# MLP weight gradients into free K/V slots, the last group finished earlier, and the MLP ahead of head 2, in an attention-plus-MLP backward kernel

## The chip, the cores and the metric

The kernel runs on one core of one Trainium2 chip. The metric is device time in microseconds (us), the median over several executions. "Span" is the length of the one profiled execution as the trace shows it; it is about 2 us shorter than the device time of the same execution.

## The reference

One decode step (one token) of attention over a cached K and V, with an MLP (SwiGLU) beside it, and then the gradients with respect to all inputs. Cut to what matters:

```python
# x, grad_out: 1x1x640; k_cache, v_cache: 1x32x8192x128; wq: 640x4096; wo: 4096x640
# w1, w3: 640x1728; w2: 1728x640; all bfloat16
xn  = layernorm(x)
q   = xn @ wq                                  # 32 heads of 128
p   = softmax(q k^T * 128**-0.5);  o = p v
h   = silu(xn @ w1) * (xn @ w3)
out = x + o @ wo + h @ w2
outputs = (out, *vjp(grad_out))   # dx, dk_cache, dv_cache, dwq, dwo, dw1, dw3, dw2
```

With one token, every large gradient is an outer product of two vectors: dK and dV are 2 MB for each of 32 heads; dw1, dw3 and dw2 are 2.2 MB each. Nearly all the time goes into moving K and V in and dK and dV out: of 304 MB moved, the four make up 268.

## The kernel before

Per head h, `phase_a` makes the scores (transposes of K on TensorE) and the softmax, `phase_t` makes the products of V with dO on VectorE, and `phase_b` overwrites the K and V tiles with dK and dV and writes them out. Loads are issued by SyncE, writes of gradients by GpSimd. There are nine 2 MB slots; a load can be issued only when its slot is free, that is, when the dK or dV that filled it has been written out. At the start the MLP's weights hold four of the nine.

```python
    kvpool = ctx.enter_context(tc.tile_pool(name="kv", bufs=9))
    tpool = ctx.enter_context(tc.tile_pool(name="tp", bufs=3))
    # ... cut ...
    load_group(0)
    load_kv(4)                      # K0 V0 K1 V1
    mD = kv_tile("mD")              # w2
    mC = kv_tile("mC")              # remainders of w1, w3, w2
    mA = kv_tile("mA")              # w1
    mB = kv_tile("mB")              # w3
    # ... loads of w2, w1, w3 cut ...
    load_kv(1)                      # K2
    # ... cut ...
    def phase_b(h):
        # ... cut ...
        for lo in range(0, J, J // 2):
            outer(Vt, doh, P2, lo, lo + J // 2)       # VectorE, line L329
        nc.gpsimd.dma_start(dvc[h], Vt[:])            # L345
        for lo in range(0, J, J // 2):
            outer(Kt, qh, U2, lo, lo + J // 2)
        nc.gpsimd.dma_start(dkc[h], Kt[:])            # L348

    def finish_group(g):            # after every fourth head: dwo, dwq and parts of out and dx
        G_ = grp.pop(g)
        # ... cut: matmuls, products on VectorE ...
        nc.gpsimd.dma_start(dwo_v[:, g * GH:(g + 1) * GH, :], wo_g[:])
        # ... cut ...
        nc.gpsimd.dma_start(dwq_v[:, :, g * GW:(g + 1) * GW], wq_g[:])

    def mlp_grads():
        oA = kv_tile("oA")
        oB = kv_tile("oB")
        oC = kv_tile("oC")
        oD = kv_tile("oD")
        d1a, d3a, d1b, d3b, d2a, d2b = split_views(oA, oB, oC, oD)
        for wi in range(2):
            bc = make_bc(wi)        # broadcast of dgate / dup: VectorE, PE, ScalarE, four steps
            da, db, dv = ((d1a, d1b, dw1_v), (d3a, d3b, dw3_v))[wi]
            for ci in range(NA):
                nc.vector.tensor_scalar(da[:, ci, :], bc[:, 0:F], xn_col[:, ci:ci + 1], None, ALU.mult)
            nc.gpsimd.dma_start(dv[:, 0:NA, :], da)
            nc.vector.tensor_scalar(db, bc[:, 0:F], xn_col[:, NA:NC], None, ALU.mult)
            nc.gpsimd.dma_start(dv[:, NA, :], db)
        for b in range(NBA):        # 12 products of dw2
            nc.vector.tensor_scalar(d2a[:, b, :], g_bc[:], hcol[:, b:b + 1], None, ALU.mult)
        # ... cut: dw2's writes, and its two last products ...

    prep_group(0)
    for h in range(2):
        phase_a(h)
        phase_t(h)
        phase_b(h)
        load_kv(2)
        if h == 0:
            load_group(1)
    phase_a(2)
    mlp()
    load_kv(4)
    phase_t(2)
    for h in range(2, H):
        # ... cut: load and prepare the next group ...
        if h + 1 < H:
            phase_a(h + 1)
            phase_t(h + 1)
        phase_b(h)
        load_kv(2)
        if hh == GH - 1:
            finish_group(g)
    # ... cut: out and dx ...
    mlp_grads()
```

## Time and profile before

| | before |
|---|---|
| device time | 766.58 us, median of 3 (765.08 to 769.03) |
| span of the profiled run | 764.5 us |
| bytes moved, mean rate | 304.35 MB, 398 GB/s |
| busy: TensorE, VectorE, ScalarE | 79%, 72%, 42% |

Below, and in all listings: PE is TensorE, PEld its weight loads, DVE VectorE, ACT ScalarE, POOL GpSimd, SP SyncE; SPq is SyncE's DMA queue. A program line is written L329.

First, the page of the kernel before: the span in 40 equal slices (19.1 us each). A digit is the mean busy share of the 16 DMA engines in tenths; below it is the rate.

```profile
DMA  8999988999999999999999999999999999999668
GB/s 344 389 428 426 415 366 328 357 424 421 411 404 401 417 425 424 430 425 420 426 430 425 416 417 424 429 424 373 412 426 426 417 359 385 401 420 389 289 270 307
```

The middle is DMA-bound. Slices 6 to 8 (95 to 153 us) and the last three are weak. The windows view of the same kernel says it in one line each. Its columns are the window and its length, then busy time and number of instructions on five engines, the granted TensorE clock, the DMA share, and GB/s.

```profile
105.00:147.00 42.00, 34.00 (x682) 29.83 (x680) 34.65 (x51) 17.56 (x26) 2.90 (x5) 0.86 0.84 321
200.00:600.00 400.00, 330.85 (x5980) 282.46 (x5981) 300.29 (x409) 185.27 (x254) 28.81 (x48) 0.79 1.01 419
```

Cut finer, the front stretch shows an empty DMA at 112.5 us:

```profile
112.50:115.00 2.50, 2.50 (x74) 2.37 (x72) 2.13 (x2) 0.16 (x1) 0.35 (x1) 1.00 0.10 39
...
122.50:125.00 2.50, 2.50 (x76) 2.49 (x73) 2.14 (x6) 2.21 (x3) 0.00 (x0) 0.98 0.92 269
125.00:127.50 2.50, 2.50 (x33) 2.16 (x32) 2.50 (x3) 2.11 (x3) 0.00 (x0) 0.50 0.96 315
```

Two timelines of the kernel before tell why. Columns: start, duration, engine, line, operation. SyncE's queue issues the loads of K5 (92.02), V5 (99.62) and K6 (100.05), and then nothing until V6 at 121.46, which waits for the write of head 2's dV; GpSimd issues that write only at 114.64, because VectorE reaches head 2's products only when the MLP is done, at 99.8 us.

```profile
92.02 0.33 SPq L123 DMA_DIRECT2D Kt<-in_A_k_cache_dram  x1
...
100.05 0.82 SPq L123 DMA_DIRECT2D Kt<-in_A_k_cache_dram  x1
121.46 0.33 SPq L123 DMA_DIRECT2D Vt<-in_A_v_cache_dram  x1
```

```profile
114.64 0.53 POOL L345 DMA_DIRECT2D out_dram<-Vt  x1 [53.75 <-DVE Vt L329]
```

The tail has two holes. Between 705 and 712.5 us everything loaded has landed and head 30's dV is not made yet; at 737.5 to 743 us the MLP gradients start from nothing. From the windows view of the kernel before:

```profile
705.00:707.50 2.50, 2.50 (x15) 1.87 (x13) 1.11 (x3) 0.10 (x2) 0.00 (x0) 0.50 0.34 144
707.50:710.00 2.50, 1.94 (x20) 1.36 (x19) 2.50 (x4) 0.00 (x0) 0.00 (x0) 0.79 0.06 26
710.00:712.50 2.50, 1.57 (x63) 1.48 (x59) 2.50 (x5) 0.00 (x0) 0.00 (x0) 0.90 0.10 33
...
737.50:740.00 2.50, 1.43 (x3) 0.20 (x2) 1.34 (x4) 1.18 (x3) 0.00 (x0) 0.50 0.10 35
740.00:742.50 2.50, 0.16 (x1) 0.00 (x0) 2.50 (x6) 0.59 (x1) 0.38 (x1) 0.50 0.00 0
```

And GpSimd's timeline there: head 30's dV and the first write of dw3 (oB):

```profile
712.56 0.53 POOL L345 DMA_DIRECT2D out_dram<-Vt  x1 [13.58 <-DVE junk L313]
...
748.41 0.88 POOL L494 DMA_DIRECT2D out_dram<-oB  x1 [4.95 <-DVE oB L493]
```

### The profile page before, as it was taken

The numbers are of one execution on the slowest core, as the hardware profiler recorded it, in microseconds if no ns is written. First come the engines' busy times: TensorE is split into PE (matmuls) and PEld (weight loads), VectorE is DVE, ScalarE is ACT, GpSimd is POOL, SyncE is SP. The second block draws the span as 40 slices with busy tenths as digits, with TensorE's granted clock in tenths as the row PEclk, the third lists the DMA queues.
The fourth block names the chain that finished last, engine by engine and source line by source line (L and its number), as shares of the span: only waits on it lengthen the run. The fifth ranks groups of instructions, "written<-read, shape, count | busy, mean of one in ns | idle before, by whom it ended". The sixth has DMA issues, their size and how long they took to land. (4 is left out here: it accounts for less than half of the span.)

```text
span 764.5 us, 23388 instructions
## 1 busy us (share of the span) xinstructions
PE 601.9 (79%) x10637; PEld 504.7 (66%) x10637; DVE 550.9 (72%) x810; ACT 323.0 (42%) x452; POOL 54.0 (7%) x95
## 2 busy tenths in 40 slices
PE   5977899599569996969768897769969798699340
PEld 3845588588458885858658676658758676687220
DVE  1792697786488888856689567866788567987963
ACT  3704246275146652725518233544418235264030
POOL 0000000100001000100001000100001000100011
PEclk9965699696587998867868678776778868697555
DMA  8999988999999999999999999999999999999668
GB/s 344 389 428 426 415 366 328 357 424 421 411 404 401 417 425 424 430 425 420 426 430 425 416 417 424 429 424 373 412 426 426 417 359 385 401 420 389 289 270 307
DMA packets 35051, 304.35 MB, mean 398 GB/s; under 512 B 2840, under 2 KB 13912, under 8 KB 18568
## 3 DMA queue, kind: packets, MB, share of 16 engines
q1 hardware_dynamic: 21828, 151.35, 48.7%
q0 software_dynamic: 12960, 151.34, 47.5%
q8 instruction: 83, 1.36, 0.7%
q10 hardware_dynamic: 164, 0.17, 0.1%
q14 instruction: 16, 0.13, 0.0%
HBM read 151.51 MB, written 151.34 MB: 396 GB/s over the span
## 5 line engine op out<-in xcount | busy, mean ns | idle before, releaser
L261 ACT COPY KT<-pT 128x1024 bf16<-128x1024 bf16 x256 | 243.1, 1036 | 53.5 <-PE pT L259 51.3
L304 PE MATMUL dp<-T,ident_bf 128*128 128x256 bf16 x1024 | 190.5, 324 | 15.1 <-DVE T L302 15.0
L302 DVE TENSOR_TENSOR T<-Vt,do_g 128x2048 bf16<-128x2048 bf16 x128 | 154.3, 1216 | 42.0 <-DMA Vt<-in_A_v_cache_dram 28.3
L259 PE MATMUL pT<-ident_bf,Kt 128*128 128x128 bf16 x2048 | 168.9, 229 | 15.2 <-DMA Kt<-in_A_k_cache_dram 15.2
L259 PEld LDWEIGHTS <-Kt 128*128 128x128 bf16 x2048 | 130.9, 103 | 20.6 <-DMA Kt<-in_A_k_cache_dram 18.0
L304 PEld LDWEIGHTS <-ident_bf 128*128 128x128 bf16 x1024 | 107.5, 115 | 41.5 <-issue 16.7
L264 PEld LDWEIGHTS <-KT 128*128 128x128 bf16 x2048 | 79.1, 98 | 36.8 <-ACT KT L261 24.0
L264 PE MATMUL sA<-qc_g,KT 128*128 128x1 bf16 x2048 | 89.2, 165 | 13.5 <-ACT KT L261 4.9
L324 ACT COPY od_g<-sA 128x2 f32<-128x2 f32 x32 | 5.1, 161 | 189.6 <-PE sA L322 166.8
L322 PEld LDWEIGHTS <-Kt 128*128 128x128 bf16 x2048 | 59.6, 101 | 31.8 <-issue 30.2
L286 PEld LDWEIGHTS <-Vt 128*128 128x128 bf16 x2048 | 57.3, 98 | 19.3 <-issue 17.3
L345 POOL DMA_DIRECT2D out_dram<-Vt x32 | 17.6, 549 | 482.9 <-DVE junk L313 190.5
L235 ACT COPY KT<-pT 128x1024 bf16<-128x1024 bf16 (+1 forms) x24 | 19.8, 874 | 40.9 <-PE pT L233 40.9
L277 ACT ACTIVATE E<-sA,negM 128x64 f32<-128x64 f32 x32 | 10.3, 321 | 63.2 <-DVE negM L274 63.0
L307 DVE TENSOR_REDUCE DP<-dp 128x64 f32<-128x256 f32 x32 | 13.3, 416 | 23.1 <-PE dp L304 23.1
L348 POOL DMA_DIRECT2D out_dram<-Kt x32 | 17.3, 542 | 147.1 <-DVE negM L274 36.0
L317 DVE COPY negD<-sA 128x1 f32<-128x1 f32 x32 | 5.0, 155 | 30.3 <-PE sA L314 30.3
L233 PE MATMUL pT<-ident_bf,wo_g 128*128 128x128 bf16 x160 | 17.0, 279 | 7.4 <-DMA wo_g<-in_A_wo_dram 7.4
L378 ACT COPY KT<-pT 128x1024 bf16<-128x1024 bf16 (+1 forms) x24 | 19.3, 877 | 2.3 <-PE pT L376 2.2
L274 DVE COPY negM<-sA 128x1 f32<-128x1 f32 x32 | 4.9, 152 | 21.1 <-PE sA L271 21.0
L233 PEld LDWEIGHTS <-wo_g 128*128 128x128 bf16 x160 | 14.5, 129 | 8.3 <-DMA wo_g<-in_A_wo_dram 7.9
L314 PE MATMUL sA<-rdot,negones_f 128*128 128x1 f32 x64 | 13.6, 282 | 7.8 <-DVE junk L313 7.8
(392 smaller groups left out, 844.6 us busy)
## 6 DMA issues: line engine op xcount, KB each, us to landing
Kt<-in_A_k_cache_dram SPq DMA_DIRECT2D x32, 2048.0 KB, 21.2
Vt<-in_A_v_cache_dram SPq DMA_DIRECT2D x32, 2048.0 KB, 23.4
out_dram<-Vt POOLq DMA_DIRECT2D x32, 2048.0 KB, 15.1
out_dram<-Kt POOLq DMA_DIRECT2D x32, 2048.0 KB, 19.9
wq_g<-in_A_wq_dram SPq DMA_DIRECT2D x8, 640.0 KB, 27.3
wo_g<-in_A_wo_dram SPq DMA_DIRECT2D x8, 640.0 KB, 24.6
out_dram<-wo_g POOLq DMA_DIRECT2D x8, 640.0 KB, 20.3
out_dram<-wq_g POOLq DMA_DIRECT2D x8, 640.0 KB, 25.3
```

The source lines that it names most:

```text
L233: nc.tensor.transpose(pT[:, k, :], wo_g[:, hh, ci * P:(ci + 1) * P], ident_bf[:])
L235: nc.scalar.copy(wT[:, 0:len(bl), :], pT[:, 0:len(bl), :])
L259: nc.tensor.transpose(pT[:, k, :], K3[:, 8 * c + k, :], ident_bf[:])
L261: nc.scalar.copy(KT[:], pT[:])
L264: nc.tensor.matmul(sA[:, j:j + 1], lhsT=KT[:, k, :], rhs=qcol, start=(j == 0), stop=True, skip_group_check=True)
L286: nc.tensor.matmul(sA[:, OC:OC + 1], lhsT=V3[:, j, :], rhs=P2[:, j, 0:1], start=False, stop=(j == J - 1), skip_group_check=True)
L302: nc.vector.tensor_tensor(T3, V3[:, :, ds_], do_h[:, ds_].unsqueeze(1).to_broadcast([P, J, QD]), ALU.mult)
L304: nc.tensor.matmul(dp[:], lhsT=ident_bf[:], rhs=T3[:, :, R * i:R * (i + 1)], start=(q == 0 and i == 0), stop=(q == DH // QD - 1 and i == Q ...
L322: nc.tensor.matmul(sA[:, OC + 1:OC + 2], lhsT=K3[:, j, :], rhs=U2[:, j, 0:1], start=False, stop=(j == J - 1), skip_group_check=True)
L345: nc.gpsimd.dma_start(dvc[h], Vt[:])
L348: nc.gpsimd.dma_start(dkc[h], Kt[:])
L378: nc.scalar.copy(wT[:, 0:len(bl), :], pT[:, 0:len(bl), :])
```

## The change

Three parts, no operation added or removed. (1) The MLP goes ahead of head 2's `phase_a`, so that its four slots come free, and VectorE gets to head 2, earlier. (2) The MLP weight gradients use slots that no further load needs: dw1 after head 29, dw3 and dw2 after head 30. (3) The last `finish_group` goes ahead of the last head's outer products, so that the last thing written is head 31's dK. The diff, cut to its core:

```diff
-        G_ = grp.pop(g)
+        G_ = grp[g]
@@ the gradients, cut
-    def mlp_grads():
+    gt = {}
+    def grads_w(wi):
+        t = kv_tile("oW")
+        v = t[:, 0:NA * F].rearrange("p (c f) -> p c f", f=F)
+        bc = make_bc(wi)
+        if wi == 0:
+            gt["C"] = kv_tile("oC")
+        tb = gt["C"][:, wi * F:(wi + 1) * F]
+        dv = (dw1_v, dw3_v)[wi]
+        for ci in range(NA):
+            nc.vector.tensor_scalar(v[:, ci, :], bc[:, 0:F], xn_col[:, ci:ci + 1], None, ALU.mult)
+        nc.gpsimd.dma_start(dv[:, 0:NA, :], v)
+        nc.vector.tensor_scalar(tb, bc[:, 0:F], xn_col[:, NA:NC], None, ALU.mult)
+        nc.gpsimd.dma_start(dv[:, NA, :], tb)
+    def grads_w2():      # cut: as before, but the two last products and their writes come first
@@ the main loop
-    phase_a(2)
     mlp()
     load_kv(4)
+    phase_a(2)
     phase_t(2)
@@
+        if h == H - 1:
+            finish_group(g)
         phase_b(h)
         load_kv(2)
-        if hh == GH - 1:
+        if h == H - 3:
+            grads_w(0)
+        elif h == H - 2:
+            grads_w(1)
+            grads_w2()
+        if hh == GH - 1 and h < H - 1:
             finish_group(g)
@@
-    mlp_grads()
```

More of the change, by code (lines that the diff above doesn't have):

```diff
@@ L481, in mlp @@
                                      start=False, stop=True, skip_group_check=True)
-    def mlp_grads():
-        oA = kv_tile("oA")
-        oB = kv_tile("oB")
-        oC = kv_tile("oC")
-        oD = kv_tile("oD")
-        d1a, d3a, d1b, d3b, d2a, d2b = split_views(oA, oB, oC, oD)
-        for wi in range(2):
-            bc = make_bc(wi)
-            da, db, dv = ((d1a, d1b, dw1_v), (d3a, d3b, dw3_v))[wi]
-            for ci in range(NA):
-                nc.vector.tensor_scalar(da[:, ci, :], bc[:, 0:F], xn_col[:, ci:ci + 1], None, ALU.mult)
-            nc.gpsimd.dma_start(dv[:, 0:NA, :], da)
-            nc.vector.tensor_scalar(db, bc[:, 0:F], xn_col[:, NA:NC], None, ALU.mult)
-            nc.gpsimd.dma_start(dv[:, NA, :], db)
-        for b in range(NBA):
-            nc.vector.tensor_scalar(d2a[:, b, :], g_bc[:], hcol[:, b:b + 1], None, ALU.mult)
-        nc.gpsimd.dma_start(out_8[0:NBA * P, :].rearrange("(fb p) c -> p fb c", p=P), d2a)
+    gt = {}
[13 more added lines that the diff above has]
+    def grads_w2():
+        t = kv_tile("oD")
+        d2a = t[:, 0:NBA * D].rearrange("p (b c) -> p b c", c=D)
+        d2b = gt["C"][:, 2 * F:2 * F + (NB - NBA) * D].rearrange("p (b c) -> p b c", c=D)
         for b in range(NBA, NB):
@@ L505, in mlp_grads @@
             nc.gpsimd.dma_start(out_8[NFULL * P:F, :], d2b[0:RB, NFULL - NBA, :])
+        for b in range(NBA):
+            nc.vector.tensor_scalar(d2a[:, b, :], g_bc[:], hcol[:, b:b + 1], None, ALU.mult)
+        nc.gpsimd.dma_start(out_8[0:NBA * P, :].rearrange("(fb p) c -> p fb c", p=P), d2a)
     prep_group(0)
```

## The prediction

Written before the changed kernel had run:

> **What bounds the kernel now.** DMA. Between 200 and 600 us the windows view gives a DMA share of 1.00 to 1.01 and 413 to 426 GB/s. The Trainium skill, "DMA: Bandwidth & Descriptors" (Specifications), puts the fabric ceiling of a core's 16 engines at 435 GB/s, and this trace's best windows (430) agree. So bytes (304.35 MB, unchanged) set a floor; only DMA idle time can be won. Windows of 2.5 to 4 us show three idle places: 108 to 136 us, about 6.5 us; 705.8 to 713 us, about 7 us; and after 737.5 us about 9 us (5.5 of them before 743.3, 2 at the end). One more, 1.7 us, at 610 us.
>
> **Why they are idle.** (1) At 112 us all issued loads have landed; the next waits for head 2's dV write, issued only at 114.6 us: phase_t of head 2 stands on VectorE behind the MLP, which ends at 99.7 us. Its gate/up matmuls run at 70 to 78 us, behind head 2's transposes, which wait for K2. (2) After 705 us the last V has been loaded, and head 30's dV is made only by 712.2 us. (3) At 737 to 743 us the MLP gradients start from nothing: four broadcast steps of 1.1 us (VectorE, PE, ScalarE) and 2.4 us of products before the first write at 742.1 us.
>
> **What the change does.** No operation is removed or added; the 7 MB of MLP gradients and their VectorE work (about 13 us: 8 broadcast steps of 0.3 to 0.43, 10 products of 0.6, 14 of 0.3) move.
> - MLP ahead of head 2: PE no longer waits for K2 before gate/up. I estimate the MLP ends on VectorE near 87 us, head 2's dV write goes out near 105 us, before DMA runs dry. Gain: 5.5 us of the 6.5, kept, because all until 700 us is DMA-bound.
> - dw1 in the 705 us hole: its products are ready near 707 to 709 us, so 3 us of idle go. But they delay head 30's outer products by some 4 us.
> - The instruction order shows a new wait: on GpSimd head 31's dV (ready near 727 us on the old clock) stands behind dw3, dw2, dwo and dwq. After head 30's dK DMA runs dry near 725 us until dw3 is ready near 730: a new hole of 4 to 6 us. From there 10 MB are queued: 25 us.
> - End: the 737 us hole goes. Last come head 31's dK (2 MB, about 5 us) and the receipt.
> Tail: about 16 us of idle become about 10, gain 6.5 us. Sum: 766.6 - 5.5 - 6.5 = 754.6, rounded to 754.
>
> **Prediction: 754 us, range 748 to 761.** Faster by over 2% (under 751.3): 0.27; within 2%: 0.72; slower: 0.01.
>
> **What would show it right or wrong.** Right: head 2's dV write issued before 108 us and no DMA share under 0.8 at 108 to 136 us; first dw1 write before head 30's dV write; one hole of 4 to 6 us before the dw3 write; last write a dK, with DMA busy without a break for 25 us before it. Wrong: the hole at 112 us still there; new idle DMA at 140 to 690 us; a hole at dw3 over 8 us or absent.
>
> **What would make it wrong.** The lead of the start could be lost again where compute limits (the hole at 610 us shows how thin the margin is), or the tail's holes could be smaller: then under 750 us. If the GpSimd order blocks longer, 758 to 760 us.

## The result, and the profile after

| | before | after |
|---|---|---|
| device time, median of 4 | 766.25 us (765.08 to 769.03) | 753.80 us (752.77 to 754.55) |
| span of the profiled run | 764.5 us | 750.6 us |
| bytes moved, mean rate | 304.35 MB, 398 GB/s | 304.35 MB, 405 GB/s |

The ratio is 0.9831, with a 95% interval of 0.9801 to 0.9862. A ratio here and below is the mean time of one kernel's runs over that of the other's of the same rounds, so it is not quite the ratio of the medians quoted. Executions over 1.5% slower than the fastest of the same kernel are left out of the means. The profiled run of after was the fastest of its four (752.77), so its span flatters the change by about 1 us.

The page of the kernel after, the same two rows (slices of 18.8 us):

```profile
DMA  8999999999999999999999999999999989999868
GB/s 346 385 427 427 415 423 427 413 406 403 423 423 423 409 429 426 423 428 418 429 428 424 420 415 423 424 426 375 426 430 425 408 316 426 425 422 412 335 216 336
```

The weak stretch at the front is gone; of the tail one very weak slice is left (216 GB/s, 713 to 732 us). The dip at 600 to 619 us (316 GB/s) was there before too (359) and is not explained here. The windows view of after for the front: the same 42 us that moved 321 GB/s now move 426, and the empty window at 112.5 us is full.

```profile
105.00:147.00 42.00, 37.08 (x729) 32.81 (x730) 33.25 (x50) 21.58 (x32) 3.23 (x5) 0.84 1.01 426
```

```profile
112.50:115.00 2.50, 2.50 (x72) 2.14 (x71) 1.15 (x4) 1.87 (x3) 0.49 (x1) 1.00 1.00 426
```

The two timelines of after that answer to those of before: K5, V5 and K6 are issued at 78.74, 83.87 and 84.30 us, 13 to 16 us earlier, and head 2's dV goes out at 102.86.

```profile
78.74 0.38 SPq L123 DMA_DIRECT2D Kt<-in_A_k_cache_dram  x1
...
84.30 0.37 SPq L123 DMA_DIRECT2D Kt<-in_A_k_cache_dram  x1
118.16 0.33 SPq L123 DMA_DIRECT2D Vt<-in_A_v_cache_dram  x1
```

```profile
102.86 0.53 POOL L345 DMA_DIRECT2D out_dram<-Vt  x1 [40.33 <-DVE U_1641 L319]
```

The tail after, windows view: a first hole at 695 us, a second at 715 us ahead of dw3, and then DMA without a break to 745 us.

```profile
692.50:695.00 2.50, 2.43 (x31) 1.92 (x28) 1.99 (x3) 1.33 (x4) 0.00 (x0) 0.86 0.54 229
695.00:697.50 2.50, 2.41 (x51) 2.20 (x52) 2.44 (x5) 2.50 (x4) 0.65 (x1) 1.00 0.11 39
697.50:700.00 2.50, 2.50 (x54) 2.26 (x52) 2.50 (x2) 2.50 (x4) 0.65 (x2) 1.00 0.78 299
...
712.50:715.00 2.50, 1.36 (x52) 1.30 (x49) 2.50 (x3) 0.17 (x2) 0.00 (x0) 0.50 0.53 223
715.00:717.50 2.50, 0.00 (x0) 0.00 (x0) 2.50 (x6) 0.00 (x0) 0.72 (x1) 0.50 0.05 20
717.50:720.00 2.50, 0.00 (x0) 0.00 (x0) 2.50 (x10) 0.00 (x0) 2.50 (x1) 0.50 0.00 0
720.00:722.50 2.50, 0.67 (x20) 0.58 (x19) 2.32 (x12) 0.00 (x0) 2.50 (x4) 0.50 0.44 174
...
725.00:745.00 20.00, 2.49 (x30) 1.75 (x27) 5.71 (x19) 1.90 (x3) 1.99 (x3) 0.50 1.01 377
```

GpSimd's timeline after, and VectorE's beside it. The dw3 write (oW) takes 4.15 us to issue, against 0.88 us before; head 31's dV, whose product VectorE ends at 714.1 us (L329), is issued at 727.92 because it stands behind dw3, dw2, dwo and dwq.

```profile
716.78 4.15 POOL L495 DMA_DIRECT2D out_dram<-oW  x1 [9.87 <-DVE oW L494]
...
727.92 0.58 POOL L345 DMA_DIRECT2D out_dram<-Vt  x1
```

```profile
711.88 2.29 DVE L329 TENSOR_TENSOR Vt<-do_g,P_13098 128x4096 bf16<-128x4096 bf16 x1
714.08 2.41 DVE L494 TENSOR_SCALAR oW<-T,xn_col 128x1728 bf16<-128x1728 bf16 x4
716.40 0.67 DVE L496 TENSOR_SCALAR oC<-T,xn_col 128x1728 bf16<-128x1728 bf16 x1
716.98 3.64 DVE L510 TENSOR_SCALAR oD<-g_bc,hcol 128x640 bf16<-128x640 bf16 x12
```

**Where the time came from.** In a DMA-bound kernel whose bytes don't change, a good measure of a lead is the time at which both traces have moved the same number of bytes (worked out by summing rate times length over 2 us windows):

| MB moved | 44 | 48 | 52 | 60 | 200 | 280 | 292 | 296 | 303 |
|---|---|---|---|---|---|---|---|---|---|
| after is ahead by, us | 0.0 | 6.3 | 8.5 | 10.2 | 10.1 | 11.7 | 14.7 | 7.2 | 14.0 |

So in these two traces about 10 us come from 109 to 157 us of the kernel before, and are kept for 500 us. Not every trace of the change keeps them: that of `after_again` (the same kernel, told below) is 10.2 us ahead at 60 MB, but 5.9 at 130 MB, 9.6 at 280 and 9.4 at 303. It has a weak stretch at 296 to 308 us (307 GB/s, where after's trace has 429). The tail (280 to 303 MB) adds 2.3 us in after's trace; the dip at 296 MB, from a lead of 14.7 us to 7.2, is the hole ahead of dw3. The prediction had 5.5 and 6.5.

### The profile page after: what moved, and what is told of

Its sections match the earlier page's. It is cut to its first block, busy times and chain, and to the rows that moved or that the text cites. A ratio compares the mean times of both kernels' runs of the same rounds, so it can differ in the third digit from the quotient of the medians.

```text
span 750.6 us, 23371 instructions
## 1 busy us (share of the span) xinstructions
PE 600.1 (80%) x10621; PEld 505.3 (67%) x10637; DVE 550.5 (73%) x810; ACT 322.0 (43%) x452; POOL 57.4 (8%) x95
## 2 busy tenths in 40 slices
DMA packets 35051, 304.35 MB, mean 405 GB/s; under 512 B 2840, under 2 KB 13912, under 8 KB 18568
## 3 DMA queue, kind: packets, MB, share of 16 engines
q0 software_dynamic: 12960, 151.34, 48.4%
HBM read 151.51 MB, written 151.34 MB: 403 GB/s over the span
## 4 chain that ended last, share of the span: by engine, by line
PE 35%; DMA 20%; issue 15%; DVE 12%; ACT 3%; POOL 1%; POOLq 0%; ACTq 0%; SPq 0%; DVEq 0%
DMA Kt<-in_A_k_cache_dram 11%; PE dp L304 11%; PE pT L259 6%; DVE Kt L329 5%; PE sA L322 4%; PE sA L286 4%; DMA Vt<-in_A_v_cache_dram 4%; PE sA L264 3%; ACT KT L261 3%; DVE Vt L329 3%; DMA out_dram<-Kt 3%; DMA wq_g<-in_A_wq_dram 3%; PE pT L376 1%; PE pF L216 1%; PE pT L233 1%
## 5 line engine op out<-in xcount | busy, mean ns | idle before, releaser
L277 ACT ACTIVATE E<-sA,negM 128x64 f32<-128x64 f32 x32 | 10.4, 325 | 70.5 <-DVE negM L274 70.3
L270 DVE TENSOR_REDUCE gmax<-sA 1x1 f32<-1x128 f32 x32 | 8.9, 277 | 15.5 <-PE sA L268 15.2
L216 PE MATMUL pF<-wq_g,xn_col_bf 128*128 128x512 bf16 x33 | 15.5, 580 | 5.2 <-DMA wq_g<-in_A_wq_dram 3.9
L376 PE MATMUL pT<-ident_bf,wq_g 128*128 128x128 bf16 x160 | 19.4, 312 | 0.0
```

What stands on the lines that cost most here:

```text
L216: nc.tensor.matmul(ps_q[:, 0:GW], lhsT=xn_col_bf[:, ci:ci + 1].to_broadcast([P, P]), rhs=wq_g[:, ci, :], start=(ci == 0), stop=(ci == NC - 1))
L376: nc.tensor.transpose(pT[:, k, :], wq_g[:, ci, hh * DH:(hh + 1) * DH], ident_bf[:])
```

## The experiments

Twelve kernels ran, all correct, in four batches; in each batch the kernel before ran beside them (medians 766.09, 766.33, 766.24 and 766.89 us). The size of a hole is its missing DMA share, summed over windows of 2.5 us.

### Which part of the change gives what

The question: is the front worth about 10 us and the tail about 3, as the traces say, or 5.5 and 6.5, as the prediction had it?

**e1: the MLP ahead of head 2, nothing else.** The kernel before with:

```diff
-    phase_a(2)
     mlp()
     load_kv(4)
+    phase_a(2)
     phase_t(2)
```

> Only the MLP goes ahead of head 2; the rest is the kernel before. Theory A (read from the bytes that DMA had moved by each moment: the changed kernel has a lead of 10 us from 150 us on, 11.7 us at 680 us): 10 to 12 us faster, 754 to 757 us, ratio 0.985 to 0.988. Theory B (my prediction's sizes: front 5.5 us, tail 6.5 us): 761 us, ratio 0.993. The lead at 200 MB tells them apart without noise of the tail: 10 us for A, 5.5 us for B.

Measured: 757.32 us, ratio 0.9898 (0.9878 to 0.9919), a gain of 7.8 us by the ratio and 8.8 by the medians. Its trace moves 416 GB/s at a share of 1.00 between 105 and 147 us. This is clearly above 5.5, and somewhat below the 10 of the traces. By the test set beforehand, the lead at 200 MB, its trace has 8.2 us (9.3 at 60 MB, 11.9 at 303): neither 10 nor 5.5, but nearer to 10. It is the trace of the fastest of six runs (754.82, 2.5 us under their median).

**e2: the changed kernel with the MLP order of before** (the edit of e1 undone in after).

> The changed kernel with the MLP back behind the transposes of head 2: both tail changes alone. Theory A: 2 to 4 us faster than before, ratio 0.995 to 0.998, with the hole ahead of the dw3 write still 7 us long. Theory B: 6.5 us faster, ratio 0.9915. If neither, then the parts do not add up.

Measured: 762.72 us, ratio 0.9964 (0.9944 to 0.9984), a gain of 2.7 to 3.4 us, well under 6.5. Its dw3 write took 4.16 us to issue, as in after, and the hole ahead of it is 7.4 us.

**e3: the last group's finish ahead of the last outer products, nothing else.** The kernel before with:

```diff
+        if h == H - 1:
+            finish_group(g)
         phase_b(h)
         load_kv(2)
-        if hh == GH - 1:
+        if hh == GH - 1 and h < H - 1:
             finish_group(g)
```

> Only the last group finished ahead of the last outer products. Theory A: nothing that DMA waits for is made earlier except dwo and dwq (1.3 MB), which now stand ahead of head 31's dV and dK; the MLP gradients still start from nothing at the end. Within 0.3% of before, ratio 0.997 to 1.003. Rival: the early finish is what lets the end overlap, then 3 us or more faster, ratio under 0.996.

Measured: 763.77 us, ratio 0.9985 (0.9960 to 1.0010). The interval holds 1: no effect that these runs resolve.

**e4: the gradients in free slots, nothing else** (after, with the MLP order and the finish of before).

> Only the MLP gradients in the slots of the last heads; last group finished at the end, MLP as before. Theory A: 0 to 4 us faster, ratio 0.995 to 1.000: one hole is filled by dw1, another opens before dw3. Rival (the gradients in the free slots carry the whole gain): 10 us faster or more, ratio under 0.987.

Measured: 762.77 us, ratio 0.9966 (0.9943 to 0.9988), the same as e2 (0.9964) within the intervals. The tail's gain is that of the gradients in free slots; dw3's issue took 4.14 us here too. The product of e1 and e2, 0.9898 × 0.9964 = 0.9862, lies within the noise of the whole (0.9831, and 0.9841 below): the parts about add up. A small interaction can't be excluded.

### Why the tail gives so little

Two costs stand in the dw3 hole: an issue of dw3 that takes 4.15 us instead of 0.8 to 0.9, and a queue order that keeps head 31's dV behind it. For the first, the Trainium skill has a mechanism: "SBUF — State Buffer", section "SBUF: two separate sides", says that a DMA issued from GpSimd needs GpSimd to write its descriptors, that VectorE and GpSimd take a shared port pair as an exclusive lock for a whole instruction, that `tensor_scalar` can take it when its operands meet further conditions (not checked here), and that a DMA issued from SyncE or ScalarE escapes this. The trace agrees as far as it goes: dw3's issue ends at 720.92 us, 0.3 us after VectorE's chain of twelve `tensor_scalar` products (716.98 + 3.64 = 720.62); in after_again, e2 and e4 it is the same 0.3 us. The rival: VectorE itself is the limit, since it is busy without a gap from 709 to 720 us, and whatever GpSimd does costs nothing.

**after_again: the changed kernel unedited**, as the measure for this batch.

> The changed kernel unaltered, to see whether its parts add up in the same session as the next runs. The two parts measured 0.9898 (MLP ahead alone) and 0.9964 (tail alone), product 0.9862, 755.5 us. If they add up: ratio 0.985 to 0.988. If the parts help each other: 0.983 again, as in the first measurement.

Measured: 754.09 us, ratio 0.9841 (0.9814 to 0.9868); dw3's issue took 4.16 us, and the hole ahead of it is 8.5 us.

**e5: the gradients' writes issued by SyncE**, whose queue has no more loads to issue there.

```diff
-        nc.gpsimd.dma_start(dv[:, 0:NA, :], v)
+        nc.sync.dma_start(dv[:, 0:NA, :], v)
@@ and the same for the four other gradient writes
```

> The changed kernel with the writes of the MLP gradients issued by SyncE instead of GpSimd; nothing else edited. Theory A (the hole of 7.5 us ahead of the dw3 write comes from GpSimd's queue: head 31's dV, ready at 714.2 us, stands behind dw3, and the issue of dw3 itself takes 4.15 us while VectorE makes the dw2 products): the hole shrinks to 2 us or less, time 5 to 7 us under the changed kernel, 747 to 749 us. Rival C (DMA runs dry because VectorE has nothing ready): hole still 4 us or more, time within 2 us of the changed kernel.

Measured: 746.94 us, ratio 0.9754 (0.9731 to 0.9778): faster than before by over 2%, and by some 7 us than after. From the timelines of e5, GpSimd's first: head 31's dV leaves at 713.66 instead of 727.92; SyncE's queue issues dw3 in 0.39 us.

```profile
713.66 0.98 POOL L345 DMA_DIRECT2D out_dram<-Vt  x1 [7.55 <-DVE Vt L329]
```

```profile
715.71 0.39 SPq L495 DMA_DIRECT2D out_dram<-oW  x1
```

The windows view of e5: of the hole ahead of dw3 one weak window is left; the next stands at a share of 1.02 and 417 GB/s.

```profile
712.50:715.00 2.50, 0.57 (x22) 0.51 (x20) 2.50 (x4) 0.16 (x1) 0.98 (x1) 0.50 0.30 119
```

The first hole shrinks too. From after to e5, 3.9 us become 2.1 in the first hole (692.5 to 700 us), and 7.5 us under 2 in the second. Together that is about 7.4 us, which is the gain. VectorE does the same work at the same place (its twelve products run 716.18 to 719.8), so the rival falls: GpSimd's queue was the cost, not VectorE's time.

**e6: the twelve dw2 products on ScalarE**, which takes away the `tensor_scalar` chain beside dw3's issue and leaves the queue order.

```diff
-            nc.vector.tensor_scalar(d2a[:, b, :], g_bc[:], hcol[:, b:b + 1], None, ALU.mult)
+            nc.scalar.activation(d2a[:, b, :], g_bc[:], ACTF.Copy, scale=hcol[:, b:b + 1])
```

> The changed kernel with the twelve large dw2 products made by ScalarE instead of VectorE; all writes still by GpSimd in the same order. Theory A1 (back-to-back VectorE tensor_scalar operations keep GpSimd from writing the descriptors of the dw3 write): the issue of the dw3 write takes under 1 us instead of 4.15, and the hole ahead of it shrinks by 3 us or more. Rival A2 (the issue waits for something else, such as room in the queue): it still takes 4 us. The total is less sure, because the products take longer on ScalarE and the dw2 write then stands ahead of head 31's dV: 0 to 4 us faster than the changed kernel.

Measured: 750.60 us, ratio 0.9802 (0.9771 to 0.9832), some 3.5 us better than after by the medians, though the intervals overlap. GpSimd's timeline of e6 (its profiled run, 757.23 us, was the slowest of six, and all lies some 8 us later): dw3's issue is short, and head 31's dV still waits at the end of the queue.

```profile
724.86 0.77 POOL L495 DMA_DIRECT2D out_dram<-oW  x1 [9.86 <-DVE oW L494]
...
734.83 0.58 POOL L345 DMA_DIRECT2D out_dram<-Vt  x1
```

So the chain beside it is what stretched the issue (0.77 against 4.15 us), and without it the hole is about 5.2 us (shares of 0.36, 0.00 and 0.56 between 720 and 727.5 us), against 7.4 to 8.5 in after, after_again, e2 and e4. From the start of dw3's issue to the end of the span it is 30.1 us, against 33.8 in after and 34.1 in after_again. Not all of this need be the issue's, because e6 also takes 3.6 us of products off VectorE. That the port pair is how the chain stretches the issue is the page's account; no run here tests it. The rest of the hole would be the order, which e9 changes.

**e9: head 31's dV made and written ahead of dw3 and dw2**, by GpSimd as in after. `phase_b` is cut into its V half and its K half:

```diff
-        phase_b(h)
+        phase_b(h, "vk" if h < H - 1 else "k")
         load_kv(2)
+        if h == H - 2:
+            phase_b(H - 1, "v")
         if h == H - 3:
```

> The changed kernel with head 31's dV product and write put ahead of dw3 and dw2; GpSimd still issues everything. It separates the two halves of the hole that the run with SyncE took away together: the order on GpSimd's queue, and the 4.15 us issue. Order theory: the dV write starts when it is ready (about 713 us), the slow issue of dw3 (expected to be 4 us again) hides behind its 5 us of transfer, and the hole is 2 us or less: as good as with SyncE, ratio 0.974 to 0.978, 746 to 749 us. Issue theory: half of the hole or more stays; ratio over 0.980.

Measured: 749.37 us, ratio 0.9773 (0.9737 to 0.9808), near e5. Head 31's dV leaves at 715.87. One expectation failed, that dw3's issue would still take some 4 us. GpSimd's timeline of e9:

```profile
721.83 0.88 POOL L497 DMA_DIRECT2D out_dram<-oW  x1 [5.42 <-DVE oW L496]
```

The same write beside the same twelve products was not stretched; here the products took the longer time instead, 3.76 us against 3.64. So e9's gain holds both the new order and the short issue, and doesn't part them. The kernel before shows that pair too (0.88 and 3.76), and so do e1 and e3. The issue was stretched in after, after_again, e2 and e4, and not in before, e1, e3 and e9: it is the same in every trace of one placement, and differs between placements. In all cases looked at (before, after, e9) the issue begins 0.38 to 0.39 us after the product ahead of the chain begins, so that start doesn't tell them apart. One thing does differ: GpSimd had been idle for 9.9 us before the issue in the four stretched ones, and for 5.0 to 5.4 us in the four others. Whether that matters was not tested; what decides it is open.

**e10: e9 with the gradients' writes by SyncE** (both edits).

> Both remedies: head 31's dV ahead of dw3 and the gradients' writes on SyncE. If both act on the same hole, as I think, they do not add: within 1.5 us of the better of the two alone, ratio 0.973 to 0.977. If they act on different waits, they add: ratio 0.970 or less.

Measured: 747.58 us, ratio 0.9747 (0.9709 to 0.9785), the same as e5. The two remedies don't add up, since they close the same hole.

### Can the gradients go still earlier?

**e8: each gradient one head earlier** (dw1 after head 28, dw3 after 29, dw2 after 30).

```diff
-        if h == H - 3:
+        if h == H - 4:
             grads_w(0)
-        elif h == H - 2:
+        elif h == H - 3:
             grads_w(1)
+        elif h == H - 2:
             grads_w2()
```

> The changed kernel with each gradient one head earlier (dw1 after head 28, dw3 after head 29, dw2 after head 30's outer products). VectorE then has less left to do when the loads are over. Theory A: the hole before dw3 goes as dw3 is written before head 30's gradients, but dw2 still stands ahead of head 31's dV: 3 to 6 us faster than the changed kernel, 748 to 751 us. Rival: the earlier writes and products delay the loads and the work of heads 30 and 31 by as much as they save: within 1.5 us of the changed kernel.

Measured: 754.12 us, ratio 0.9835 (0.9817 to 0.9852): no gain over after. VectorE's timeline of e8 shows a likely reason, which no run tests alone: the slot for the second tile was not free yet, and VectorE, which works in program order, stood 9.17 us behind it:

```profile
688.51 0.67 DVE L496 TENSOR_SCALAR oC<-T,xn_col 128x1728 bf16<-128x1728 bf16 x1 [9.17 <-DMA out_dram<-Vt]
```

**e12: e5 with the large part of dw2 after head 28** (`grads_w2` cut in two, its twelve products first of all), a candidate for a better kernel.

> A candidate for best: the SyncE kernel with the large part of dw2, which needs one slot only, made already after head 28, while DMA still has loads. The run with all gradients one head earlier stalled VectorE 9.2 us for a second slot; this one asks for none. If the two holes left in the SyncE kernel (about 2 us each at 693 and 713 us) are there because VectorE is behind, then 2 to 4 us faster than it, 743 to 745 us, ratio 0.970 to 0.973. If VectorE's 3.6 us of dw2 products merely move ahead and delay head 29 to 31 by as much, the same as the SyncE kernel, 747 us, ratio 0.974 to 0.977.

Measured: 752.51 us, ratio 0.9811 (0.9772 to 0.9851), worse than e5. VectorE's timeline of e12 shows the same kind of stall: the first of the twelve products, at 675.62 us, had waited 7.73 us for the write of a dK to free the slot.

### What the front was waiting for

**e11: head 2's `phase_t` ahead of the MLP, in the kernel before.** If head 2's dV write is all that DMA waits for at 112 us, getting VectorE to head 2 first should do at least as well as the change. The rival: the MLP's four slots must come free early as well.

```diff
     phase_a(2)
+    phase_t(2)
     mlp()
     load_kv(4)
-    phase_t(2)
```

> The kernel before with phase_t of head 2 also put ahead of the MLP, so that the MLP stands behind head 2 as a whole instead of in the middle of it. Tail as before. Theory A (what counts is that head 2's dV write is issued before DMA has landed all loads at 110 us): head 2's dV goes out near 87 us, the hole at 110 to 145 us goes although the MLP ends later than in either kernel; 6 to 10 us faster, ratio 0.987 to 0.992. Rival (what counts is that the MLP ends early, so that its four slots are free for the loads of heads 4 to 6): the MLP ends near 105 us, those loads come later still, and DMA idles somewhere between 95 and 125 us; no faster, ratio 0.997 or more.

Measured: 769.10 us, ratio 1.0034 (0.9996 to 1.0071): no gain, so my theory fell. Head 2's dV was written even earlier than in after, at 98.25 us against 102.86, and the kernel was no faster. SyncE's queue of e11 issued nothing between K4 (77.96 us) and V4 (100.35 us): V4 takes a slot of the MLP, which now came late.

```profile
77.96 0.36 SPq L123 DMA_DIRECT2D Kt<-in_A_k_cache_dram  x1
100.35 0.33 SPq L123 DMA_DIRECT2D Vt<-in_A_v_cache_dram  x1
```

DMA ran empty from 92.5 us until some 99, as the windows view of e11 shows:

```profile
92.50:95.00 2.50, 2.50 (x61) 1.80 (x58) 1.46 (x1) 0.28 (x2) 0.00 (x0) 1.00 0.06 26
95.00:97.50 2.50, 0.02 (x1) 0.00 (x0) 2.44 (x3) 0.00 (x0) 0.00 (x0) 1.00 0.00 0
```

The hole moved from 112 us to 95 us (and there is another at 147.5 to 150 us, with a share of 0.10). The run advanced one thing and delayed the other: K5, V5 and K6 were issued 13 to 19 us later than before. So it shows that an early dV is not enough when the MLP's slots come late. What fits both runs is that the MLP-first order frees both: the MLP's slots (K5, V5 and K6 issued 13 to 16 us earlier) and, soon after, head 2's. A kernel with early slots and a late dV was not run, so what each is worth stays open.

## Why the prediction was right or wrong

**The total was right, and two wrong terms made it so.** It said 754 us (748 to 761), within 2%; measured were 753.8 and, again, 754.09.

- **The bound.** Right: DMA. The "DMA: Bandwidth & Descriptors" page (Specifications) of the Trainium skill gives a fabric ceiling of 435 GB/s; 419 before and 421 after, over 400 us, lie just under it.
- **The front's mechanism.** Right in its steps: the MLP ends on VectorE at 84.2 us (estimated 87), dV of head 2 leaves at 102.86 (estimated 105, "before 108"), no share under 0.8 between 108 and 136 us, and in after's trace nothing of it lost in the middle. In after_again's trace the front is the same, but some 4 us of the lead are lost at 296 to 308 us (the share is 0.71 from 300 to 304). The prediction had called the lead "kept", and had named such a loss as what could make it wrong.
- **The front's size.** Wrong: "Gain: 5.5 us of the 6.5". The failed step is that only the missing DMA *share* was counted as winnable. Over 105 to 147 us the missing share is 16% of 42 us, 6.7 us. But the rate was 321 GB/s, and 426 could be had: (426 − 321)/426 × 42 = 10.4 us. The difference lies in windows such as 122.5 to 127.5 us, with shares of 0.92 and 0.96 and rates of 269 and 315. The trace's lead is 10.1 us; alone (e1) the part measured 7.8 to 8.8 us.
- **The front's cause.** Half right: the next load indeed waited for head 2's dV, but e11 shows that an early dV gives nothing when the MLP's slots come later for it.
- **The tail's mechanism.** Right: dw1's first write (696.85 us) precedes head 30's dV (700.91), head 31's dV stands behind dw3, dw2, dwo and dwq, there is a hole ahead of dw3, and the last write is a dK with some 25 us of unbroken DMA up to its end (busy from about 721.4 to 747).
- **The tail's size.** Wrong: "gain 6.5 us" measured 2.7 to 3.4 us (e2). "A new hole of 4 to 6 us" measured 7.5 us, and 8.5 in after_again, over the 8 us that the prediction itself had set as wrong. The failed step is that its sum has no term for dw3's issue, which takes 0.88 us in the trace of before; beside the chain of dw2's products it took 4.15 us. Without the chain (e6) the hole is 5.2 us, inside the predicted range. This term accounts for at most 2 to 3 of the 3 to 4 us that are missing; the rest is not accounted for. The last `finish_group`'s place, to which the sum gave no term of its own, has no effect that shows (e3).
- **The sum.** Front too small by 2 to 3 us as measured in e1 (by 5 in the trace's rates), tail too large by 3 to 4 us. They cancelled. A right total is no proof of its terms; here only e1 and e2 showed it.

**Still open:** what decides whether GpSimd's issue or VectorE's chain yields; why some traces lose 1 to 4 us of the front's lead in the middle and others don't (e1's falls from 9.5 us at 120 MB to 8.2 at 130), which is the size of the difference between the lead of 10 us and the gain in e1; and how much of the front each of the two kinds of slot is worth.

**A better version.** The gradients' writes on SyncE (e5, 746.94 us) beats both kernels; e10 (747.58 us) is equal to it and more complicated.

## What to carry to other kernels

Where DMA is the bound, size a hole by the bytes that were not moved at the rate seen elsewhere in the same trace, not by the missing busy share, and compare two versions by the time at which they have moved the same bytes, in more than one trace of each. Late writes that depend on nothing else belong on a DMA queue that is idle and in the order in which their data come ready; on a GpSimd queue a ready write waits behind an unready one, and its issue can be stretched by VectorE's work. Work moved ahead into a "free" slot must find it free at that moment, or the engine that fills it stalls in program order (9.17 us in e8, 7.73 in e12).

## What the Trainium skill lacked or had wrong

- "SBUF — State Buffer" (section "SBUF: two separate sides") says that the shared pair is held for one instruction and that whichever starts first gets it. If the pair is the cause, dw3's issue was held here through a chain of twelve `tensor_scalar` instructions (4.15 us, ended 0.3 us after the chain), not one; and with the issue beginning 0.38 to 0.39 us after the same preceding product, it was stretched in after and not in before and e9 (0.88 us, where the chain took 3.76 instead of 3.64 us). By these starts, the page's rule does not tell which happens.
- The same page's remedy, issuing from another queue, held in e5: 0.39 us for the same write from SyncE, which was over just before the chain began, and 1.24 us for the write after it, beside the chain (1.25 us for the same write of dw1, without a chain). It doesn't mention another gain that came with it here, that writes on GpSimd's queue no longer wait behind it (head 31's dV 14 us earlier).
- "DMA: Bandwidth & Descriptors" (Specifications) gives an HBM limit of about 358 GB/s for a core beside the 435 of the fabric, and the table doesn't say when it holds; the same page's note to its measured rates (section "Bandwidth") does: with both cores of a pair streaming. With this one core running, 419 to 421 GB/s were held over 400 us (reads and writes are 151.51 and 151.34 MB in the whole run), so the note holds and the table alone would mislead.
- "Perfetto Trace Analysis" (section "Identifying the Most-Contended Engine") says that for DMA the busy share misleads because there are 16 engines, but not by how much. Here 269 and 315 GB/s went with shares of 0.92 and 0.96, against 419 at 1.01. The cause was not tested.
